# Another order of the first operations of a planned attention and MoE kernel, with 48 casts, copies and squares moved between ACT and DVE

## The chip, the cores and the metric

The kernel runs on one core of a Trainium2 chip. A core has five engines that this text calls PE (matrix multiplication), DVE (vector), ACT (scalar), POOL and SP. Each runs its own list of instructions strictly in the order in which the program gives them, and waits where an instruction needs a result that another engine or a transfer has not delivered. SP only issues transfers between HBM and on-chip memory. The metric is the time of one execution on the device in microseconds, as a median of several runs.

## The reference, cut to what matters

A linear attention with random features, and behind it a gated product with weights `w_a`, `w_b` and `w_out`:

```python
batch, n_heads, seq, head_dim, n_features = 8, 8, 576, 64, 128
n_tokens, d_model, d_ff = 4608, 512, 1536

def phi(x):
    proj = np.einsum('bhsd,md->bhsm', x, omega)
    sq = np.sum(x * x, axis=-1, keepdims=True) / 2.0
    h = proj - sq
    h = h - np.max(h, axis=-1, keepdims=True)
    return np.exp(h) / np.sqrt(m)
q_p, k_p = phi(q * scale), phi(k * scale)
kv = np.einsum('bhsm,bhsd->bhmd', k_p, v)
z = np.sum(k_p, axis=2)
num = np.einsum('bhsm,bhmd->bhsd', q_p, kv)
den = np.einsum('bhsm,bhm->bhs', q_p, z)[..., None] + 1e-06
x = num / den                      # then 4608 tokens x 512
out = ((x @ w_a) * (x @ w_b)) @ w_out
```

The weights come as 64-bit numbers, everything else as 32-bit.

## The kernel before

**Units.** The attention is cut into 32 units, one per batch and pair of heads; names end in the batch and the pair, so that `sm_0_1` belongs to batch 0, pair 1. A unit loads `X` (features in rows) and `natk`, `natq` (tokens in rows). `square_sums` (L557) squares a `nat` tile in place on ACT (L560) and sums it on DVE (L562). In the first pair of heads the squares come from `X` itself (L611) and PE sums them (L616). PE projects with `om` into `ppk` and `ppq` (L574), DVE takes maxima (L627) and forms the biases `sm` (L634, L635), and ACT computes the exponentials `hk` and `hq` (L640).

**The first four units** go through `tok_tail` (L964): PE transposes `hq` into `pq` (L957), a copy brings that to `qT`, PE forms `pkv` (L980) and `pn` (L994), DVE divides (L999 to L1006) into `x32t` and `tails`, PE transposes `x32t` into `px` (L1013), and `split` (L519) makes two halves of the result: `x` high, a cast (`copier`, L392), and `x` low, the subtraction of that cast (`subber`, L404). Each matrix product of the MoE is three PE products of such halves. Later units get their denominators through POOL and a small trip through HBM (`z_sums`, L792), and their transposition through another (`turn`, L881).

**Weights.** `convert` (L436) turns each 64-bit piece `raw` into 32-bit high and low halves: two ACT steps (L446, L448), one DVE step (L450), a cast that may be done by ACT (L396) or DVE (L398), and a subtraction on DVE (L404). There are 36 pieces, 24 of `wa` and `wb` and 12 of `wo`. The `raw` tiles share their memory with tiles that are used later or earlier, so a load has to wait until the last reader of the former tile is done.

**MoE.** The first two batches go through `moe_block` (L1232): for each of 12 steps, PE computes `pa` and `pb` (L1250, four groups of three products each over `x_0` to `x_3`), ACT copies `pa` to `a`, DVE multiplies (L1258) and splits the product into `ghl` high and low, and PE adds four groups of output products `o` (L1060). Batches from the third on use sums of weights and activations with seven products in place of eight (L1343, L1353).

**The order.** Nothing is written in the order in which it runs. The functions describe operations to a `Graph` (L60), each with a cost per engine that may do it, a due number and the tiles it reads and writes. `plan` (L313) runs a list scheduling of all engines and of the transfers, gives each operation one engine and each tile one place in memory, and returns the operations sorted by their planned start. The kernel then issues them in that sequence, so that each engine's list and SP's are cut out of one row of 5637 operations. What an instruction must wait for is worked out from the tiles when it is issued.

Of the kernel before, what the change touches and what calls it, by code (L numbers as in the profile page):

```python
# [352 lines left out]
def tile_attention_moe(ctx: ExitStack, tc: tile.TileContext, kqt, kqtt, kqn, kqnt, vx, omst, idn, wab, wout, out):  # L356
    nc = tc.nc
# [106 lines left out]
    for n, (kind, i, w) in enumerate(units):  # L464
        pr = 4000 + n * 4000 / len(units)
# [91 lines left out]
    def square_sums(src, sq, n, nm, pr, b, alloc_sq):  # L557

        for nat, o, part in src:
            g.op({"ACT": act(n * D)}, lambda e, nat=nat: nc.scalar.activation(nat.ap[:], nat.ap[:], AF.Square, scale=SQ),  # L560
                 r=[(nat, None)], w=[(nat, None)], prio=pr, margin=0 if b < 2 else CFG["LOAD"])
            g.op({"DVE": dve(n * D)}, lambda e, nat=nat, o=o: nc.vector.tensor_reduce(o(), nat.ap[:], axis=X, op=ALU.add),  # L562
                 r=[(nat, None)], w=[(sq, part)], alloc=[sq] if part in (0, None) else [], prio=pr)
# [529 lines left out]
    class Out7:  # L1093
# [26 lines left out]
        def product(self, key, A, W, prio, end, part=None):  # L1120

            n = self.n[key] = self.n.get(key, -1) + 1
            free = key in (1, 0)
            pb = spare[key] if free else self.acc[key]
            begin, stop = (key == 1 or n == 0), (key == 1 or end)

            def go(e):
                for t in range(2) if part is None else (part,):
                    for j, (ai, wi) in enumerate(((0, 0), (0, 1), (1, 0))):
                        nc.tensor.matmul(pb.ap[:, t], A[0](ai)[:, t * P:(t + 1) * P], W[0](wi), start=begin and t == j == 0, stop=stop and t == 1 and j == 2)  # L1130
            g.op({"PE": mm(6 if part is None else 3, HM)}, go, r=[*A[1], *W[1]], w=[(pb, 0), (pb, 1)] if part is None else [(pb, part)],
                 alloc=[pb] if n == 0 and not free else [], prio=prio)
            return pb
# [324 lines left out]
    for b in range(B + 1):  # L1458
# [3 lines left out]
        else:  # L1462
            if b == B:

                for hp in range(NHP):
# [3 lines left out]
                         prio=-20, nbytes=P * SM * 4)  # L1469
# [6 lines left out]

    order = g.plan()
    with tc.manual_schedule():  # L1480
        for o in order:
            for b in o.alloc:
# [70 lines left out]
```

## Time and profile before

| what | value |
|---|---|
| median of 3 runs | 1042.24 µs (1042.18 to 1042.42) |
| the profiled execution's own time | 1041.62 µs |
| its span from first to last instruction | 1039.8 µs |
| mean granted TensorE clock | 0.998 |
| POOL busy | 114.0 µs (11%) |
| transfers | 314.44 MB, 302 GB/s on average |
| largest share of the chain that ended last | PE, 79% |
| next in that chain | DVE 8%, ACT 1% |

The share of busy time says how much of the span an engine had an instruction running. PE's ends are modelled, so that a busy PE isn't PE at its peak. Idle time in a row stands in front of the instruction that ended it, with the engine or transfer that had been waited for.

### The profile page before, as it was taken

The page shows a single profiled execution, that of the slowest core. Times are in us where ns is not written, and L with a number is a line of the kernel's source. Part 1 is how long each engine was busy: PE and PEld are TensorE (multiplying, and loading weights), DVE is VectorE, ACT ScalarE, POOL GpSimd, SP SyncE. Part 2 cuts the span into 40 slices and gives each one's busy share as a digit, 9 for nine tenths or more (in the row PEclk, how much of TensorE's full clock was granted, in tenths as well). Part 3 has the DMA queues.
Part 4 walks back from the last instruction along what each step waited for, and adds up shares of the span by engine and source line. Part 5 has one row for each costly group of instructions (what it writes and reads, how often), then busy time and mean ns, then how long its engine had stood idle before and what let it go on. Part 6 is the DMA issues. An engine that isn't in the chain of part 4 may idle for free.

```text
span 1039.8 us, 26266 instructions
## 1 busy us (share of the span) xinstructions
PE 1024.4 (99%) x9902; PEld 897.0 (86%) x9902; DVE 887.3 (85%) x2212; ACT 598.4 (58%) x1656; POOL 114.0 (11%) x181
## 2 busy tenths in 40 slices
PE   9899999999999999999999999999999999999998
PEld 7677777777788888988888888888899899999998
DVE  6999999899999888878887978888876579998766
ACT  8997798677665665566565656665454123332211
POOL 0032211120111111111101111111110000000000
PEclk9999999999999999999999999999999999999999
DMA  9877879989899998999989988989888888899981
GB/s 352 308 281 239 285 242 307 304 331 317 298 349 363 307 317 294 315 330 313 306 275 351 310 300 296 339 303 309 272 288 268 268 320 313 318 344 341 371 303 47
DMA packets 123665, 314.44 MB, mean 302 GB/s; under 512 B 17681, under 2 KB 40977, under 8 KB 123537
## 3 DMA queue, kind: packets, MB, share of 16 engines
q1 hardware_dynamic: 122656, 312.10, 86.5%
q8 instruction: 78, 1.28, 0.5%
q10 hardware_dynamic: 880, 0.66, 0.2%
q14 instruction: 51, 0.41, 0.1%
HBM read 255.52 MB, written 57.18 MB: 301 GB/s over the span
## 4 chain that ended last, share of the span: by engine, by line
PE 79%; DVE 8%; ACT 1%; issue 1%; DVEq 0%; ACTq 0%
PE p L1343 39%; PE o L1060 19%; PE o_P L1130 5%; PE pa L1250 3%; PE pb L1250 3%; PE pkv L849 3%; PE pm L917 2%; PE ppk L594 1%; PE p L594 1%; DVE sm L627 1%; DVE c L1353 1%; PE p L1130 1%; DVE zero L868 1%; PE ppk L574 1%; PE ppke L574 1%
## 5 line engine op out<-in xcount | busy, mean ns | idle before, releaser
L1353 DVE TENSOR_TENSOR c<-p,c 128x512 f32<-128x512 f32 (+1 forms) x336 | 207.7, 618 | 67.9 <-PE p L1343 59.4
L1060 PE MATMUL o<-wo,ghl 128*128 128x512 f32 x1008 | 258.5, 397 | 0.4 <-DVE ghl L404 0.3
L1060 PEld LDWEIGHTS o<-wo,ghl 128*128 128x128 f32 x1008 | 181.0, 188 | 39.9 <-issue 4.7
L1343 PE MATMUL p<-Sa,t 128*128 128x256 f32 x1008 | 132.6, 281 | 0.0
L1343 PEld LDWEIGHTS p<-Sa,t 128*128 128x128 f32 x1008 | 124.6, 188 | 0.4 <-issue 0.2
L802 POOL TENSOR_TENSOR z<-hk 128x256 f32<-128x256 f32 x56 | 44.5, 795 | 607.7 <-ACT hk L640 431.3
L396 ACT CAST ghl<-c 128x512 fp32r<-128x512 f32 (+1 forms) x75 | 42.5, 579 | 100.5 <-DVE c L1403 80.9
L878 ACT ACTIVATE hq<-hq,dn 128x128 f32<-128x128 f32 x224 | 71.1, 392 | 29.1 <-DVE dn L874 28.9
L868 DVE CUSTOM_DVE_ANT_0 zero<-hq,zb 128x128 bf16<-128x128 f32 x224 | 79.5, 355 | 4.9
L1250 PE MATMUL pa<-x,wa 128*128 128x512 f32 x288 | 75.9, 406 | 3.6 <-ACT wa L396 2.0
L1343 PE MATMUL p<-Sb,bq 128*128 128x256 f32 x504 | 74.1, 283 | 0.0
L1343 PE MATMUL p<-x,t 128*128 128x256 f32 x504 | 74.0, 282 | 0.0
L1250 PE MATMUL pb<-x,wb 128*128 128x512 f32 x288 | 73.3, 398 | 0.4 <-DVE a L1258 0.4
L1343 PE MATMUL p<-Sb,t 128*128 128x256 f32 x504 | 73.5, 282 | 0.0
L396 ACT COPY c<-p 128x256 f32<-128x256 f32 x84 | 31.3, 372 | 73.0 <-PE p L1343 62.3
L1343 PEld LDWEIGHTS p<-x,wa 128*128 128x128 f32 x504 | 64.9, 188 | 7.2 <-DVE c L1353 3.7
L1343 PE MATMUL p<-x,wa 128*128 128x256 f32 x504 | 68.2, 283 | 2.0 <-DVE c L1353 1.0
L1250 PEld LDWEIGHTS pa<-x,wa 128*128 128x128 f32 x288 | 53.6, 191 | 19.0 <-ACT a L396 2.2
L640 ACT ACTIVATE hq<-hq,sm 128x128 f32<-128x128 f32 x192 | 65.4, 392 | 7.4 <-DVE sm L635 6.0
L1343 PEld LDWEIGHTS p<-x,wb 128*128 128x128 f32 x504 | 64.6, 188 | 3.8 <-DVE c L1353 0.6
L1343 PE MATMUL p<-x,wb 128*128 128x256 f32 x504 | 67.7, 282 | 0.1
L1343 PEld LDWEIGHTS p<-x,t 128*128 128x128 f32 x504 | 65.8, 189 | 1.6 <-DVE c L1353 0.4
(209 smaller groups left out, 2019.6 us busy)
## 6 DMA issues: line engine op xcount, KB each, us to landing
t<-td SPq DMA_DIRECT2D x168, 512.0 KB
wo<-wod SPq DMA_DIRECT2D x96, 512.0 KB
bq<-bd SPq DMA_DIRECT2D x84, 256.0 KB
qdr<-qd SPq DMA_DIRECT2D x112, 160.0 KB
hq<-qdr SPq DMA_DIRECT2D x28, 640.0 KB
X<-in_kqt_dram SPq DMA_DIRECT2D x30, 512.0 KB
raw<-in_wab_dram SPq DMA_DIRECT2D x24, 512.0 KB
td<-ts SPq DMA_DIRECT2D x24, 512.0 KB
```

The costliest lines, as they stand in the source:

```text
L396: nc.scalar.copy(o(), i())
L574: nc.tensor.matmul(pps[w].ap[half, c * M:c * M + M], x()[rows, c * P + D * t:c * P + D * t + D], om.ap[rows], start=True, stop=True)
L640: g.op({"ACT": 392}, lambda e, c=c, w=w, to=to, at=at: nc.scalar.activation(to.ap[:, at + c], src[w](c), AF.Exp, scale=SC, bias=sm.ap[:, 2 ...
L802: g.op({"POOL": pool2(n)}, lambda e: nc.gpsimd.tensor_tensor(o(), a(), c(), op=ALU.add), r=r, w=w, alloc=list(al), prio=pri, deps=zload[-1 ...
L849: nc.tensor.matmul(pkv.ap[D * j + d:D * j + d + Q, 0:M], vb.ap[:, vc, d:d + Q], c(), start=(n == 0), stop=(n == 4))
L868: g.op({"DVE": 413}, lambda e, c=c, j=j, rr=rr, qc=qc: nc.vector.tensor_tensor_reduce(out=junk.ap[rr], in0=qc(), in1=zb.ap[rr, j], scale=1 ...
L878: g.op({"ACT": 392}, lambda e, c=c, src=src: nc.scalar.activation(hq.ap[:, c], src(), AF.Copy, scale=dn.ap[:, c:c + 1]), r=[sd, (dn, None) ...
L1060: nc.tensor.matmul(po.ap[:], ghl.ap[:, gi, t * P:(t + 1) * P], wo.ap[:, wi], start=(n == 0 and i == 0), stop=(n == NF - 1 and i == 2))
L1130: nc.tensor.matmul(pb.ap[:, t], A[0](ai)[:, t * P:(t + 1) * P], W[0](wi), start=begin and t == j == 0, stop=stop and t == 1 and j == 2)
L1250: nc.tensor.matmul(pb.ap[:], wt.ap[:, wi, c], xs[c].at(xi), start=(c == 0 and i == 0), stop=(c == NC4 - 1 and i == 2))
L1343: nc.tensor.matmul(pb.ap[:, half], wcol(wi, c), xc(xi, c), start=n == 0, stop=n == 5)
L1353: g.op({"DVE": dve(n)}, lambda e: nc.vector.tensor_tensor(c4.ap[:, o], pb.ap[:, half], y(), op=ALU.add), r=[*((pb, k) for k in range(half. ...
```

## The change

Two tables of numbers and a function are added, and the sequence that the planner returns goes through that function. `OTHER` names places in the planner's sequence and an engine for each: 26 operations go from ACT to DVE, and 22 from DVE to ACT. They are the casts of weights (`convert`), the copies of `qT`, casts of `ghl`, copies of finished outputs, and the two squares of L611. `AFTER` has 1411 pairs; a pair (i, j) puts the operation at place i of the planner's sequence right behind the one at place j. Operations that aren't named keep their sequence. The highest place named is 2115, and the last 3311 of the 5637 operations stand where they stood. Places in memory are those the planner gave.

`square_sums` also gets a variant for POOL, which runs only where an operation has POOL as its engine. `OTHER` names DVE and ACT alone, so it runs nowhere. Line numbers grow by 25 to 30: L627 of before is L657 now, L562 is L590, L404 is L429, L398 is L423, L450 is L475, L611 is L641 (642 on DVE), L1250 is L1280 and L1060 is L1090.

```diff
+OTHER = ((27,"DVE"),(37,"DVE"),(99,"DVE"),(100,"DVE"),(131,"ACT"),(136,"DVE"),(169,"DVE"),
...
+AFTER = ((6,8),(5,9),(16,5),(15,20),(14,15),(13,24),(18,13),(37,40),(48,42),(57,45),(61,57),
...
+def arranged(order):
+
+    for i, e in OTHER:
+        order[i].eng = {e: 0}
+    moved = {i for i, _ in AFTER}
+    follow = {}
+    for i, j in AFTER:
+        follow[j] = i
+    got = []
+
+    def put(i):
+        while i is not None:
+            got.append(i)
+            i = follow.pop(i, None)
+    put(follow.pop(-1, None))
+    for i in range(len(order)):
+        if i not in moved:
+            put(i)
+    return [order[i] for i in got]
...
-            g.op({"ACT": act(n * D)}, lambda e, nat=nat: nc.scalar.activation(nat.ap[:], nat.ap[:], AF.Square, scale=SQ),
-                 r=[(nat, None)], w=[(nat, None)], prio=pr, margin=0 if b < 2 else CFG["LOAD"])
-            g.op({"DVE": dve(n * D)}, lambda e, nat=nat, o=o: nc.vector.tensor_reduce(o(), nat.ap[:], axis=X, op=ALU.add),
+            s = g.op({"ACT": act(n * D)}, lambda e, nat=nat: nc.scalar.activation(nat.ap[:], nat.ap[:], AF.Square, scale=SQ) if e == "ACT" else
+                     nc.gpsimd.tensor_tensor(nat.ap[:], nat.ap[:], nat.ap[:], op=ALU.mult),
...
-    order = g.plan()
+    order = arranged(g.plan())
```

DVE's list near its start, where unit 1 ends and unit 2 begins, before (`sm_1` and `sm_2` are the biases of pairs 1 and 2, `rd_00` the first division):

```order
L627 TENSOR_REDUCE sm_1_307<-ppk_14_335 128x4
L627 TENSOR_REDUCE sm_1_307<-ppq_14_336 128x4
L634 SCALAR_TENSOR_TENSOR sm_1_307<-sm_1_307,sq_1_324 128x2x4
L627 TENSOR_REDUCE sm_1_307<-ppq_10_304 128x4
L627 TENSOR_REDUCE sm_2_416<-ppk_20_412 128x4
L627 TENSOR_REDUCE sm_2_416<-ppq_20_413 128x4
L999 TENSOR_SCALAR rd_00_437<-pn_00_436 128x5
```

The same place of DVE's list now:

```order
L657 TENSOR_REDUCE sm_1_281<-ppq_14_324 128x4
L657 TENSOR_REDUCE sm_1_281<-ppk_14_323 128x4
L423 COPY qT_0_273<-pq_01_390 128x384
L590 TENSOR_REDUCE sq_2_401<-natk_2_153 128x8
L423 COPY qT_0_273<-pq_02_396 128x384
L657 TENSOR_REDUCE sm_2_412<-ppk_20_408 128x4
L657 TENSOR_REDUCE sm_2_412<-ppq_20_409 128x4
L1029 TENSOR_SCALAR rd_00_430<-pn_00_429 128x5
```

Ahead of the first maximum of unit 2 there now stand two copies of `qT` that ACT did before, and a sum of squares that stood further back.

PE's list in the first MoE batch, around the fifth step (`pa_4`, `pb_4`), before; `o_0` to `o_3` are the four outputs, and the number behind `ghl` is the step it comes from:

```order
L1060 MATMUL o_0_1098<-wo_1154,ghl_2_1315 128x512 x3
L1060 MATMUL o_1_1106<-wo_1154,ghl_2_1315 128x512 x3
L1060 MATMUL o_2_1118<-wo_1154,ghl_2_1315 128x512 x3
L1060 MATMUL o_3_1159<-wo_1154,ghl_2_1315 128x512 x3
L1250 MATMUL pa_4_1467<-x_0_530,wa_1255 128x512 x3
L1250 MATMUL pa_4_1467<-x_1_713,wa_1255 128x512 x3
L1250 MATMUL pa_4_1467<-x_2_829,wa_1255 128x512 x3
L1250 MATMUL pa_4_1467<-x_3_935,wa_1255 128x512 x3
L1250 MATMUL pb_4_1499<-x_0_530,wb_1345 128x512 x3
```

The same place now:

```order
L1280 MATMUL pb_4_1469<-x_1_732,wb_1334 128x512 x3
L1280 MATMUL pa_4_1399<-x_2_833,wa_1331 128x512 x3
L1090 MATMUL o_3_1087<-wo_1313,ghl_3_1441 128x512 x3
L1280 MATMUL pb_4_1469<-x_2_833,wb_1334 128x512 x3
L1090 MATMUL o_1_1251<-wo_1225,ghl_2_1316 128x512 x3
L1280 MATMUL pa_4_1399<-x_3_929,wa_1331 128x512 x3
L1090 MATMUL o_0_1095<-wo_1313,ghl_3_1441 128x512 x3
L1280 MATMUL pb_4_1469<-x_3_929,wb_1334 128x512 x3
```

Output groups of two steps stand singly between the groups of `pa` and `pb`, which alternate; some outputs of step 3 stand ahead of the end of step 4's first products, and before they stood behind all of them.

SP's list around the load of the fifteenth weight piece, before (`raw_972`) and now (`raw_1123`):

```order
L407 DMA raw_972<-in_wout_dram 128x512
L407 DMA xtd<-xts_571 128x4x64
L407 DMA X_1_978<-in_kqt_dram 128x1024
L407 DMA natq_1_984<-in_kqn_dram 128x512
L407 DMA raw_996<-in_wab_dram 128x512
```

```order
L432 DMA raw_1073<-in_wout_dram 128x512
L432 DMA raw_1121<-in_wab_dram 128x512
L432 DMA raw_1123<-in_wout_dram 128x512
L432 DMA X_1_1125<-in_kqt_dram 128x1024
L432 DMA zdr_87<-zx_0_1188 8x32
L432 DMA zb_0_1214<-zdr_87 128x256
```

`X_1_978` of before is `X_1_1125` now. The load `raw_1121` (the twentieth piece) now stands ahead of both; before it stood 15 rows behind the fifteenth.

More of the change, by code (lines that the diff above doesn't have):

```diff
@@ L42 @@
 CFG = dict(PORT=0.5, EDF=("DVE", "ACT", "POOL"), STEP=15000, LOOK=60000, NOISE=(200, 600), CHOSEN=((858009,0,387055,152612,0,0,0,715321,0,0,680034,0,0,0,0,780129,689749,0,892332,0,0,84647,0,0,0,0,0,0,0,0,0,0,0,0,0,0,0,0,0,0,0,0,0,0,0,0,0,0,0,0,0,0,0,0,0,0,0,0,0,0,0,0,0,0,0,0,0,0,0,0),), ZS=800, ZB=(300, 1600, 3600), ZD=(300, 1600, 3100), HQ=(1100, 2600, 3600), BACK2=(300, 1100, 2600), TW=(), XL=["v0", "v1", "Xt0", "ht2", "hq0"], OWR=["raw0", "raw1"], ONE=((7, 1),), SAFE=500, OWN=16, OWNU=(), HOLD=1000, TG=1, G4=4, WAIT=150, RAW=600, FAST=(0, 1, 2, 3), JOIN0=False, WARM=8, HROOM=["w0", "u1", "w1", "u2", "w2", "u3"], H=3, TURN=(7,), BACK=1500, AT=2, GATES=(-4, -1, 2, 5), SQPE=4, MARGIN=1200, LOAD=1100, SUMS=1000, NATS=(1, 2, 3), CONV=(28000, 2600))
+OTHER = ((27,"DVE"),(37,"DVE"),(99,"DVE"),(100,"DVE"),(131,"ACT"),(136,"DVE"),(169,"DVE"),(219,"DVE"),(224,"ACT"),(242,"DVE"),(259,"ACT"),(269,"DVE"),(270,"ACT"),(284,"DVE"),(352,"ACT"),(354,"ACT"),(355,"DVE"),(402,"DVE"),(447,"ACT"),(449,"ACT"),(475,"ACT"),(494,"ACT"),(560,"ACT"),(562,"ACT"),(674,"ACT"),(683,"DVE"),(707,"ACT"),(708,"ACT"),(736,"ACT"),(801,"DVE"),(813,"DVE"),(973,"ACT"),(976,"DVE"),(1006,"DVE"),(1070,"ACT"),(1081,"DVE"),(1142,"DVE"),(1218,"DVE"),(1331,"DVE"),(1403,"ACT"),(1498,"ACT"),(1709,"DVE"),(1848,"ACT"),(1862,"DVE"),(1866,"DVE"),(1939,"DVE"),(1950,"ACT"),(2049,"DVE"),)
@@ L559, in square_sums, with total @@
         for nat, o, part in src:
-            g.op({"ACT": act(n * D)}, lambda e, nat=nat: nc.scalar.activation(nat.ap[:], nat.ap[:], AF.Square, scale=SQ),
-                 r=[(nat, None)], w=[(nat, None)], prio=pr, margin=0 if b < 2 else CFG["LOAD"])
-            g.op({"DVE": dve(n * D)}, lambda e, nat=nat, o=o: nc.vector.tensor_reduce(o(), nat.ap[:], axis=X, op=ALU.add),
-                 r=[(nat, None)], w=[(sq, part)], alloc=[sq] if part in (0, None) else [], prio=pr)
+            s = g.op({"ACT": act(n * D)}, lambda e, nat=nat: nc.scalar.activation(nat.ap[:], nat.ap[:], AF.Square, scale=SQ) if e == "ACT" else
+                     nc.gpsimd.tensor_tensor(nat.ap[:], nat.ap[:], nat.ap[:], op=ALU.mult),
+                     r=[(nat, None)], w=[(nat, None)], prio=pr, margin=0 if b < 2 else CFG["LOAD"])
+            def total(e, nat=nat, o=o, s=s):
+                nc.vector.tensor_reduce(o(), nat.ap[:], axis=X, op=ALU.add)
+                if "POOL" in s.eng:
+                    nc.gpsimd.tensor_scalar(o(), o(), SQ2, 0.0, op0=ALU.mult, op1=ALU.add)
+            g.op({"DVE": dve(n * D)}, total, r=[(nat, None)], w=[(sq, part)], alloc=[sq] if part in (0, None) else [], prio=pr)
     def four(nm, b, pri, x, xdep, dst, c0, sm, sq, al, deps, mg, more):
```

1 line of the change is left out of this document (added).

## The prediction

> **What bounds the kernel now.** I read the totals first and then the table of windows, since the change ends near 450 µs and an average over the whole span says little about that stretch. A window's columns are the stretch, its length, the busy time and instruction count of PE, PEld (weight loads), DVE, ACT and POOL, the granted clock, the DMA share and GB/s.
>
> ```profile
> PE 1024.4 (99%) x9902; PEld 897.0 (86%) x9902; DVE 887.3 (85%) x2212; ACT 598.4 (58%) x1656; POOL 114.0 (11%) x181
> ...
> 0.00:25.00 25.00, 22.96 (x441) 17.79 (x445) 17.18 (x44) 20.71 (x65) 1.19 (x11) 1.00 0.93 351
> 25.00:50.00 25.00, 21.19 (x319) 16.81 (x311) 23.05 (x59) 24.19 (x63) 0.40 (x2) 0.93 0.83 308
> 50.00:75.00 25.00, 24.31 (x220) 18.80 (x220) 24.79 (x51) 24.51 (x63) 6.06 (x8) 1.00 0.87 305
> 75.00:100.00 25.00, 24.64 (x194) 19.01 (x193) 24.77 (x76) 20.01 (x54) 8.13 (x10) 1.00 0.66 209
> 100.00:125.00 25.00, 24.64 (x239) 18.38 (x242) 24.77 (x58) 18.80 (x52) 5.54 (x6) 1.00 0.83 289
> 125.00:450.00 325.00, 322.84 (x3037) 267.38 (x3025) 293.58 (x781) 223.77 (x623) 47.54 (x72) 1.00 0.91 313
> 450.00:1040.00 590.00, 583.82 (x5488) 538.80 (x5476) 479.14 (x1148) 266.40 (x742) 45.09 (x72) 1.00 0.86 298
> ```
>
> PE is idle for 2.04 + 3.81 = 5.85 µs up to 50, for 0.69 + 0.36 + 0.36 = 1.41 from 50 to 125, and for 2.16 from 125 to 450, 9.4 in all. The change takes no work off PE, so the order can win only idle time and time at a low clock. The low clock of 0.93 sits in one place:
>
> ```profile
> 36.00:38.00 2.00, 1.18 (x32) 0.94 (x32) 1.66 (x3) 2.00 (x7) 0.20 (x1) 1.00 0.96 381
> 38.00:40.00 2.00, 0.51 (x18) 0.37 (x14) 1.83 (x3) 2.00 (x6) 0.00 (x0) 1.00 0.67 254
> 40.00:42.00 2.00, 1.49 (x4) 0.97 (x5) 2.00 (x6) 2.00 (x5) 0.00 (x0) 0.85 0.05 20
> 42.00:44.00 2.00, 2.00 (x6) 1.51 (x6) 1.93 (x6) 2.00 (x5) 0.00 (x0) 0.50 0.87 295
> 44.00:46.00 2.00, 2.00 (x9) 1.59 (x8) 1.92 (x5) 2.00 (x5) 0.00 (x0) 0.80 0.57 229
> ```
>
> Two poorly filled windows (1.18 and 0.51 of 2 µs) are followed by 2 × (0.15 + 0.50 + 0.20) = 1.7 µs of lost clock. With the 9.4 that makes **11.1 µs, the ceiling** of what the order can bring, unless PE's matmuls also stand closer than their modelled ends show. In these windows DVE and ACT are full, and DVE stays full (24.8 of 25) to 125. So up to about 125 µs I take the time from DVE's list: PE waits for what DVE and ACT hand over.
>
> **The change part by part.** *DVE's first work.* The timeline gives start, duration, instruction, and the idle time before it with what ended it.
>
> ```profile
> 3.97 0.63 ACT L611 ACTIVATE x<-X 128x512 f32<-128x512 f32 x1 [1.00 <-DMA X<-in_kqt_dram]
> 6.26 0.63 ACT L611 ACTIVATE x<-X 128x512 f32<-128x512 f32 x1 [0.84 <-DMA X<-in_kqt_dram]
> 5.38 0.69 DVE L627 TENSOR_REDUCE sm<-ppk 128x4 f32<-128x512 f32 x1 [4.44 <-PE ppq L574]
> 17.17 0.69 DVE L627 TENSOR_REDUCE sm<-ppk 128x4 f32<-128x512 f32 x1 [1.51 <-PE ppq L574]
> 20.39 0.55 DVE L398 COPY qT<-pq 128x384 f32<-128x384 f32 x1
> 20.85 0.67 DVE L562 TENSOR_REDUCE sq<-natk 128x8 f32<-128x512 f32 x1
> 21.44 0.68 DVE L562 TENSOR_REDUCE sq<-natq 128x8 f32<-128x512 f32 x1
> ```
>
> DVE idles until 5.38. Now its first row is a square that ACT did at 3.97, as soon as X had landed; DVE so has work from 3.97, which wins 5.38 − 3.97 = 1.4. Against it stands SP's new order, with one more load of 128x512 (0.26 MB) ahead of the second half of X. At the 351 GB/s of the first window that is 0.75 µs. The half landed by 6.26, and DVE wants it for its second square after one square, two maxima and two small steps, near 3.97 + 1.8 + 0.4 = 6.2. So it costs between 0 (if that load lands beside others) and 0.75; I take 0.4, the middle, since neither row is nearer. *First work: +1.0.*
>
> *The hole at 17.17.* DVE waits 1.51 for PE there. Its new list has two copies of `qT` and a sum of squares in front of this reduction. From start to start a copy takes 20.85 − 20.39 = 0.46 and a sum 21.44 − 20.85 = 0.59, together 1.51. Useful work fills the hole: *+1.5*, between 0 (if `pq` isn't there yet) and 1.51; I take the upper end because PE's `pq` product stands ahead in its list.
>
> *Waits for ACT's casts.*
>
> ```profile
> 31.93 0.69 DVE L404 TENSOR_TENSOR x<-px,x 128x512 fp32r<-128x512 f32 x1 [0.26 <-ACT x L396]
> 38.16 0.69 DVE L404 TENSOR_TENSOR x<-px,x 128x512 fp32r<-128x512 f32 x1 [0.48 <-ACT x L396]
> 40.02 0.42 DVE L398 CAST wb<-raw 128x512 fp32r<-128x512 f32 x1
> 40.36 0.16 DVE L999 TENSOR_SCALAR rd<-pn 128x5 f32<-128x5 f32 x1
> 47.86 0.69 DVE L404 TENSOR_TENSOR x<-px,x 128x512 fp32r<-128x512 f32 x1 [0.37 <-ACT x L396]
> 50.54 0.68 DVE L404 TENSOR_TENSOR wa<-raw,wa 128x512 fp32r<-128x512 f32 x1
> ```
>
> They are 0.26 + 0.48 + 0.37 = 1.1 µs. ACT's list ahead of the last of these casts is 15 rows shorter and 5 longer, so ACT comes earlier, but DVE comes earlier too. Between 0 and 1.1 I take half, *+0.6*.
>
> *Length of DVE's list.* Counted in the two lists with 0.59 for a sum, maximum, square or subtraction, 0.46 for a copy and 40.36 − 40.02 = 0.34 for a cast: ahead of the subtraction at 50.54 stand 4.7 µs of work that were not there and 5.0 fewer, *+0.3*. If reading `pq` and `raw` on DVE beside busy ACT costs more than these rows, it is between −1 (a fifth on 4.7) and +0.3; I keep +0.3.
>
> At 50 µs that makes 1.0 + 1.5 + 0.6 + 0.3 = **3.4**, of PE's 5.85 idle and 1.7 of clock, so there is room for it.
>
> The clock alone can spoil this. By the rows above, windows with PE a quarter to a half busy were enough, and PE was never idle for more than 2.0 µs in a row, as its waits show:
>
> ```profile
> 37.12 1.39 PE L994 MATMUL pn<-kvz,qT 128*64 128x66 f32 x40 [0.82 <-ACT kvz L396]
> 40.51 3.95 PE L1250 MATMUL pa<-x,wa 128*128 128x512 f32 x9 [2.00 <-ACT wa L396]
> ```
>
> If the gap at 40.51 shrinks with the earlier hand-over, the dip goes too and PE can follow DVE's full gain. The Trainium skill ("TensorE: Matmul & The Clock Gate", Part 1, "What's actually happening") puts the half clock behind an idle window of about 3.4 µs that runs freely. By that rule the dip would not hang on this 2.00 µs gap and could come back at another place; the trace here speaks for the row, with a dip behind a shorter gap, and the sum by the rule would be 1.7 lower.
>
> *From 50 to 125.* Ahead of the first low half of `ghl` in the fourth step DVE's list has 12 rows more (5.3 µs) and 20 fewer (9.2), 3.9 shorter; in the seventh step it is 2.7 shorter (6.0 against 8.7). DVE being full there, PE could be handed its data that much earlier, but PE has only 1.41 of idle left: *+1.4*, from 0 (PE is bound by itself) to 1.4. I take the upper end as DVE's surplus is over twice as large.
>
> *From 125 to 450.* PE's idle 2.16 in many small waits; its operations are moved up to 354 µs, by at most 16 places. Between −2.2 (as much new idle as there was) and +2.2; half, *+1.0*, since the moves put single output groups between waiting products. Behind that nothing is moved.
>
> *Sum:* 3.4 + 1.4 + 1.0 = 5.8. The profiled execution took 1041.62 (span 1039.8 and 1.8 around it), so 1035.8; the median of the runs stands 0.62 higher: **1036.4**.
>
> **The rivals.** *ACT takes over as the bound.* ACT has 24.51 of 25 busy from 50 to 75, and between 51 and 100 its list grows by 6 rows net.
>
> ```profile
> 62.15 0.65 ACT L396 CAST wa<-raw 128x512 fp32r<-128x512 f32 x1
> 62.70 0.71 ACT L448 ACTIVATE raw<-raw 128x512 int32<-128x512 uint32 x1
> 63.30 1.24 ACT L446 ACTIVATE raw<-raw 128x512 f32<-128x512 f32 x2
> 83.02 0.66 ACT L446 ACTIVATE raw<-raw 128x512 f32<-128x512 f32 x1 [1.26 <-DMA raw<-in_wab_dram]
> ```
>
> At 62.70 − 62.15 = 0.55 each, that is 3.3: of the 3.4 nothing much is left, and with the late 1.0 the median is 1042.24 − 1.1 = 1041.1. Against it: from 0 to 51 ACT's list is 2.8 shorter, and from 75 on ACT has 5 of 25 free.
>
> *The slower one: SP's list stops behind one load.* SP issues in order. The load of the twentieth piece waits for the last reader of the memory that it reuses, the low half of the fourth `wa` piece, which is the last of these four:
>
> ```profile
> L404 DVE TENSOR_TENSOR wa<-raw,wa x4: 676/688/692, 40.5 to 62.8; 128x512 fp32r<-128x512 f32 x4
> ...
> 47.30 0.42 SPq L407 DMA_DIRECT2D raw<-in_wout_dram  x1
> 63.55 0.36 SPq L407 DMA_DIRECT2D raw<-in_wab_dram  x1
> 78.27 0.33 SPq L407 DMA_DIRECT2D raw<-in_wab_dram  x1
> ```
>
> It was issued at 63.55, right after that subtraction ended (62.8 + 0.7). Now the fifteenth piece, issued at 47.30 before and read by ACT at 63.30, stands behind it, and so do X of the next batch and the transfers of `z`. The load issued at 78.27 kept ACT waiting until 83.02, so one lands about 4.7 µs after its issue. If the subtraction still ends at 63.5, the fifteenth piece is there at 63.5 + 0.4 + 4.7 = 68.6, 5.3 after ACT wanted it; ACT stands still, and with it every `ghl` behind it. DVE would have gained nothing by then; less the late 1.0 that is +4.3, a median of 1046.5. It begins to cost when the subtraction ends after 63.30 − 4.7 − 0.4 = 58.2. I expect 63.5 − 3.4 (gained at 50) − 2.5 (DVE's list ahead of it is shorter by that) = 57.6, close to the edge, but ACT's reader also stands 9 rows further back in ACT's list, about 9 × 0.55 = 5 µs of cover.
>
> *A smaller gain:* the hole at 17 and the first work only move the wait to ACT or to X; then 0.6 + 0.3 + 1.4 + 1.0 = 3.3, and 1038.9. *A larger gain:* the dip goes and the small waits too, up to the ceiling of 11.1: 1031.1. That the change does nothing can be excluded: 1411 of 5637 places differ in the lists.
>
> **How the numbers follow.** About 0.2% (2.1 µs) is what a measurement of this kernel can tell from no change. Forecast, a gain of 4 to 9 µs: 0.50. Larger gain, above 9: 0.11. Smaller, 2.1 to 4: 0.15. ACT as the bound, within 0.2%: 0.13. SP's stop, slower by more than 0.2%: 0.11. Faster so has 0.50 + 0.11 + 0.15 = 0.76. The range has to leave out no more than 2 in 10: from the ceiling, 1031.0, to 1043.0, which takes in the smaller gain and ACT's case, and leaves out most of the slower case and of what might lie beyond the ceiling.
>
> **What would show it.** DVE's first row after the memset starts near 4.0; no wait above 0.3 µs is left near 17; the first `pa` product of the MoE starts before 38.5, and the window 42 to 44 shows clock 1.00; PE's idle from 25 to 50 falls from 3.81 to under 2; from 450 on PE's busy and idle time stay as they were, only earlier. The slower rival would show as SP waiting before the load of the twentieth piece and ACT waiting for `raw` near 60 µs; ACT's case as DVE and PE waiting for ACT's `ghl` or `wa` casts from 50 to 75. The prediction is wrong if PE's time is lost between matmuls that stand close already, so that the idle that goes comes back as longer spacing, or if DVE's copies and casts take longer beside ACT than in the rows used.

## The result, and the profile after

The changed kernel takes 1054.17 µs (median of 4 runs, 1052.92 to 1054.74) against 1042.26 before, a ratio of 1.0112 with a 95% interval of 1.0095 to 1.0130. It is 11.9 µs slower, and the prediction had said 5.8 µs faster. The profiled execution took 1052.92 µs (span 1051.1), the shortest of the four.

The windows of the changed kernel, with the columns of before:

```profile
0.00:25.00 25.00, 22.93 (x414) 17.40 (x418) 19.34 (x50) 19.96 (x64) 1.13 (x10) 1.00 0.93 345
25.00:50.00 25.00, 23.94 (x373) 19.49 (x368) 24.63 (x65) 25.00 (x69) 0.95 (x3) 1.00 0.84 312
50.00:75.00 25.00, 24.75 (x257) 19.28 (x253) 23.85 (x55) 23.57 (x58) 8.93 (x13) 1.00 0.63 218
75.00:100.00 25.00, 23.84 (x154) 17.09 (x156) 23.40 (x63) 23.08 (x58) 4.46 (x7) 1.00 0.80 270
100.00:125.00 25.00, 24.35 (x249) 18.29 (x250) 24.26 (x66) 19.54 (x55) 4.59 (x7) 1.00 0.86 292
125.00:450.00 325.00, 314.94 (x2891) 257.99 (x2890) 287.82 (x756) 215.62 (x599) 46.19 (x72) 0.99 0.88 304
450.00:1040.00 590.00, 588.97 (x5539) 543.52 (x5539) 481.94 (x1160) 269.93 (x754) 45.60 (x72) 1.00 0.88 303
```

From 25 to 50 PE idles 1.06 µs where it idled 3.81, and the clock is full. From 75 on it goes the other way: 1.81 idle from 75 to 125 (0.72 before), and 10.06 from 125 to 450 (2.16 before). DVE, which had 24.8 of 25 from 50 to 125, has 23.4 to 24.3 now. The engines are *less* busy and the work takes longer, so waits have been added.

**Position at equal PE work.** To see where, I matched the two traces operation by operation (both hold the same 1320 groups on PE), gave each kind of group the start-to-start time that its fastest tenth has in the kernel before, and summed these up along each kernel's own list. The table says how much later (+) or earlier (−) each kernel begins the same amount of PE work than the kernel before, with the first projection of each trace put at the same time; up to 0.9 µs of the first column is a start that differs from one execution to the next (e2, e6 and e16 begin with the old lists). Each row is one execution; e15's was 1.3 µs longer than the median of its runs, the change's 1.3 shorter. Kernels of the experiments are in it too.

| before is at | 25 | 55 | 80 | 125 | 200 | 250 | 450 | 1030 |
|---|---|---|---|---|---|---|---|---|
| the change | 0.8 | −5.8 | −5.7 | −3.1 | 0.1 | 7.0 | 9.7 | 11.2 |
| e1: new order for 400 operations | 1.0 | −5.5 | −1.2 | −1.1 | −0.4 | −0.4 | −0.1 | 1.6 |
| e2: new order behind 400 | 0.9 | 0.4 | 0.4 | 2.1 | 5.3 | 13.3 | 16.1 | 15.8 |
| e3: swaps alone | 0.1 | 0.4 | 2.3 | 2.3 | 3.9 | 5.7 | 7.3 | 7.1 |
| e4: order alone | 6.9 | 2.0 | 5.8 | 11.5 | 19.2 | 24.5 | 28.1 | 29.8 |
| e5: SP's list by readiness | 1.7 | −4.6 | −4.5 | −1.8 | 6.4 | 12.1 | 23.3 | 25.4 |
| e6: new order behind 1000 | 0.9 | 0.4 | 0.4 | 0.4 | 2.6 | 5.9 | 8.3 | 8.0 |
| e7: new order for 1000 | 1.8 | −4.7 | −4.7 | −2.2 | 6.0 | 6.0 | 6.8 | 8.3 |
| e8: new order for 300 | 1.3 | −2.2 | −2.1 | −3.2 | −3.1 | −3.2 | −2.8 | −1.4 |
| e13: eleven rows ahead | 1.2 | −5.3 | −5.2 | −2.8 | 2.8 | 7.8 | 12.3 | 13.7 |
| e14: 116 rows ahead | 1.4 | −5.1 | −3.1 | 3.1 | 9.6 | 16.4 | 24.6 | 26.0 |
| e15: the change, DVE light | 1.0 | −5.5 | −5.2 | −4.0 | −2.2 | 2.1 | 1.8 | 3.1 |
| e16: the old order, DVE light | 0.9 | 0.0 | 0.0 | −1.6 | −1.9 | −2.4 | −2.6 | −3.1 |

The change is 5.8 µs ahead at 55, holds that to 80, and then loses 15.4 until 450, and another 1.5 slowly behind it, where nothing was moved.

**What the loss looks like.** All waits of PE from 125 to 450 (engine, line and tile waited for, µs in total, times, longest), before:

```profile
PE p L1343 <- ACT hk L396: 0.8, 1, 0.8
PE pa L1250 <- ACT a L396: 0.7, 1, 0.7
PE o L1060 <- DVE ghl L404: 0.3, 1, 0.3
PE ppq L594 <- ACT k L396: 0.2, 1, 0.2
```

and now:

```profile
PE pb L1280 <- DVE a L1288: 2.5, 3, 1.9
PE ppk L624 <- DVE x L429: 1.7, 2, 1.0
PE ppk L604 <- DVE x L429: 1.4, 1, 1.4
PE ppq L604 <- DVE x L429: 1.4, 2, 0.9
PE p L1373 <- ACT hk L421: 0.7, 1, 0.7
PE ppq L624 <- ACT k L421: 0.7, 1, 0.7
PE p L1373 <- DVE Sa L429: 0.5, 1, 0.5
PE pa L1280 <- ACT a L421: 0.4, 1, 0.4
PE o L1090 <- DVE ghl L429: 0.4, 1, 0.4
```

That is 2.0 µs in 4 waits against 9.7 in 13, and no single one carries it. PE's idle time grows by 7.9 in this stretch and a half-clock stretch near 250 takes 1.7, together 9.6 of the 12.8 µs that the table has from 125 to 450. The other 3.2 stand in neither: the same groups of products take longer from start to start. PE's ends are modelled, and where those 3.2 lie wasn't looked into. The largest wait, 1.94 at 248.90, shows the manner. The product `a` of DVE releases the bank that the next `pb` writes to. The timelines of DVE and PE in the changed kernel:

```profile
240.62 0.29 DVE L898 CUSTOM_DVE_ANT_0 zero<-hq,zb 128x128 bf16<-128x128 f32 x1 [2.31 <-ACT hq L670]
...
247.82 0.29 DVE L898 CUSTOM_DVE_ANT_0 zero<-htq,zb 64x128 bf16<-64x128 f32 x1
248.04 0.08 DVE L898 DVE_READ_ACCUMULATOR2_ANT dn<- 64x1 f32 x1
248.15 0.69 DVE L1288 TENSOR_TENSOR a<-pb,a 128x512 f32<-128x512 f32 x1
...
246.46 0.49 PE L1090 MATMUL o<-wo,ghl 128*128 128x512 f32 x1 [0.38 <-DVE ghl L429]
248.90 0.97 PE L1280 MATMUL pb<-x,wb 128*128 128x512 f32 x3 [1.94 <-DVE a L1288]
```

DVE first stands 2.31 for `hq` and `zb` (put down to ACT, whose first `hq` of this unit was done at 236.4; the load of `zb`, issued at 233.2, is the likelier releaser, as its semaphore rose at 240.48), then works through rows of the denominators, and comes to the product 4 µs after its inputs are there. PE then loses the 1.94 and a half-clock stretch behind it. On the chain of waits that ended last, the pieces of transfers sum to 50 µs from 60 to 350 (17 to 130, 9 to 200, 24 to 350). Before there is none, as far as that chain goes back, to 104. By line, for the window 200 to 350, before and now:

```profile
by line: PE p L1343 19.0%; PE o L1060 16.0%; PE pa L1250 8.8%; PE pb L1250 7.4%; PE pkv L849 4.1%; issue 3.9%; DVE zero L868 3.2%; DVE wr L1281 2.9%; PE pm L917 2.9%; DVE ts L404 2.9%; DVE sm L627 2.8%; ACT hq L640 2.4%; ACT hq L878 1.8%; D
```

```profile
by line: PE p L1373 7.4%; DVE zero L898 7.0%; DMA td<-ts 6.0%; issue 5.7%; DMA qdr<-qd 5.6%; PE o L1090 5.6%; DMA zb<-zdr 4.5%; DMA X<-in_kqt_dram 3.6%; ACT hq L908 3.5%; DVE ts L429 3.3%; PE pb L1280 3.2%; PE pa L1280 3.0%; DVE sq L590 2.7
```

Before, the chain runs mostly through PE. Now it hops between DVE, PE, transfers and ACT, and none of these works through.

### The profile page after: what moved, and what is told of

The parts are those of the page before. It is cut to its first block, busy times and chain, and to the rows that moved or that the text cites. A ratio compares the mean times of both kernels' runs of the same rounds, so it can differ in the third digit from the quotient of the medians.

```text
span 1051.1 us, 26233 instructions
## 1 busy us (share of the span) xinstructions
PE 1030.2 (98%) x9902; PEld 899.3 (86%) x9902; DVE 891.2 (85%) x2216; ACT 597.1 (57%) x1652; POOL 111.8 (11%) x181
## 4 chain that ended last, share of the span: by engine, by line
PE 70%; DVE 15%; DMA 8%; ACT 4%; issue 2%; SPq 1%; DVEq 0%; ACTq 0%
PE p L1373 37%; PE o L1090 17%; PE o_P L1160 4%; PE pkv L879 2%; DMA raw<-in_wab_dram 2%; DVE zero L898 2%; PE pm L947 2%; PE ppk L624 1%; PE p L624 1%; PE pb L1280 1%; DMA zb<-zdr 1%; DVE raw L475 1%; DVE c L1383 1%; DMA qdr<-qd 1%; PE pa L1280 1%
## 5 line engine op out<-in xcount | busy, mean ns | idle before, releaser
L1090 PE MATMUL o<-wo,ghl 128*128 128x512 f32 x1008 | 265.2, 397 | 0.4 <-DVE ghl L429 0.4
L1090 PEld LDWEIGHTS o<-wo,ghl 128*128 128x128 f32 x1008 | 180.9, 188 | 39.5 <-issue 4.3
L1373 PE MATMUL p<-Sa,t 128*128 128x256 f32 x1008 | 135.0, 282 | 0.5 <-DVE Sa L429 0.5
L1373 PEld LDWEIGHTS p<-Sa,t 128*128 128x128 f32 x1008 | 127.0, 189 | 1.5 <-DVE Sa L429 0.7
L1280 PE MATMUL pa<-x,wa 128*128 128x512 f32 x288 | 81.6, 405 | 1.0 <-ACT a L421 1.0
L1280 PE MATMUL pb<-x,wb 128*128 128x512 f32 x288 | 79.3, 399 | 3.2 <-DVE a L1288 2.5
L1373 PE MATMUL p<-Sb,t 128*128 128x256 f32 x504 | 74.1, 283 | 0.0
L1373 PE MATMUL p<-x,t 128*128 128x256 f32 x504 | 73.8, 282 | 0.0
L1373 PE MATMUL p<-Sb,bq 128*128 128x256 f32 x504 | 73.7, 282 | 0.0
L1373 PEld LDWEIGHTS p<-x,wa 128*128 128x128 f32 x504 | 65.0, 189 | 7.3 <-DVE c L1383 4.0
L1373 PE MATMUL p<-x,wa 128*128 128x256 f32 x504 | 68.6, 283 | 1.9 <-DVE c L1383 1.0
L670 ACT ACTIVATE hk<-hk,sm 128x128 f32<-128x128 f32 x184 | 63.2, 392 | 10.7 <-DVE sm L665 6.9
L1280 PEld LDWEIGHTS pb<-x,wb 128*128 128x128 f32 x288 | 52.8, 188 | 18.6 <-DVE a L1288 4.6
L1373 PEld LDWEIGHTS p<-x,wb 128*128 128x128 f32 x504 | 64.8, 188 | 3.8 <-DVE c L1383 0.7
L1373 PE MATMUL p<-x,wb 128*128 128x256 f32 x504 | 67.7, 282 | 0.1
```

The lines of the kernel that those rows point to most:

```text
L670: g.op({"ACT": 392}, lambda e, c=c, w=w, to=to, at=at: nc.scalar.activation(to.ap[:, at + c], src[w](c), AF.Exp, scale=SC, bias=sm.ap[:, 2 ...
L1090: nc.tensor.matmul(po.ap[:], ghl.ap[:, gi, t * P:(t + 1) * P], wo.ap[:, wi], start=(n == 0 and i == 0), stop=(n == NF - 1 and i == 2))
L1280: nc.tensor.matmul(pb.ap[:], wt.ap[:, wi, c], xs[c].at(xi), start=(c == 0 and i == 0), stop=(c == NC4 - 1 and i == 2))
L1373: nc.tensor.matmul(pb.ap[:, half], wcol(wi, c), xc(xi, c), start=n == 0, stop=n == 5)
```

## The experiments

### Early or late part, swaps or order

Kernel e1 takes the new order for its first 400 operations only, e2 for all the others:

```diff
+    was = {i: order[i].eng for i, _ in OTHER}
     for i, e in OTHER:
         order[i].eng = {e: 0}
...
+    head = set(got[:400])
+    for i in was: order[i].eng = order[i].eng if i in head else was[i]
-    return [order[i] for i in got]
+    return [order[i] for i in got[:400] + sorted(set(got) - head)]
```

> The new order (with the engines that it gives) for its first 400 operations, which end near 57 us; behind them all operations in the old order with their old engines. Compared at equal PE work, the change was 5.7 us ahead of before at 55 us and 9.7 us behind at 450. Theory A (the loss sits in the new lists from 60 us on, above all in SP's, where loads now stand behind waiting transfers): the 5.7 stays, 1036 to 1038. Theory B (whatever is won early is given back, since weights and loads don't come earlier and DVE is full to 125 us): 1041 to 1043. Theory C (the early order leaves something behind that costs later): 1046 or more.

```diff
+    head = set(range(400))
+    for i in was: order[i].eng = was[i] if i in head else order[i].eng
-    return [order[i] for i in got]
+    return [order[i] for i in sorted(head) + [i for i in got if i not in head]]
```

> The first 400 operations in the old order with their old engines, the rest as the change has it. Theory A: the loss of 5.7 + 9.7 = 15.4 us between 55 and 450 is there without the early gain, near 1057. Theory B: the loss was the gain given back plus some, 1046 to 1052. Theory C: near 1042, since what harms is left out.

e1 took 1043.09 (ratio 1.0012, interval 1.0002 to 1.0022), e2 1056.50 (1.0137, 1.0122 to 1.0153). e1 lies at the upper edge of theory B's range, e2 at theory A's figure. The table says more than the times. e2 starts with the old lists, has no early gain, and loses 15.7 from 55 to 450, as much as the change. **So the loss belongs to the new lists behind the 400th operation, with or without the early gain**; that settles theory C against the early part. In e1 the gain of 5.5 is there until 65 µs and 4.3 of it goes in one place, at the seam, where DVE, ACT and PE stand together (PE 2.60 for `a`, and a half-clock stretch). So theory A's 1037 doesn't come, and what takes the gain is the seam, not the weights and loads of theory B.

The two halves of the change alone: e3 has `return order` in place of the last line, e4 an empty loop over `OTHER`.

```diff
-    for i, e in OTHER:
+    for i, e in ():
```

> The 48 changes of engine alone, all lists in the old sequence. Theory A: the swaps matter little beside SP's list, 1040 to 1046. If the engine swaps make the loss (theory D: work on ACT or DVE where it is waited for), 1050 or more.

> The new sequence alone, each operation on its old engine. Theory A: most of the loss stays, 1050 to 1058. Theory D (the swaps make the loss): 1036 to 1044.

e3 took 1048.68 (1.0063, 1.0048 to 1.0078) and e4 1072.18 (1.0290, 1.0265 to 1.0315). Both miss: e3 lies between the two theories, e4 far above both, and theory D falls with it. Swaps alone cost 6.4 µs, the order alone 30, and together 11.9. The two prices don't add up, so neither half has a price of its own. A likely reason, argued and not shown, is that the order is written for these swaps, and without them the engines meet rows whose work stands on another engine.

### Is it SP's list?

> The lists of PE, DVE, ACT and POOL as the change has them, row for row. Only SP's list differs: a transfer is put where its memory and its data were ready in the trace of the change, but not before the time at which it was issued in the kernel before; 394 operations move in the sequence, and X of unit 2 of the third batch, issued at 195.1 us after 37 us behind waiting transfers, comes ahead near 160. Theory A (SP's list makes the loss): at least half of the 15.4 us come back, 1047 or less. Theory E (the loss is in the lists of DVE, ACT and PE, and transfers only show it): 1051 to 1056.

The edit is another table `AFTER`, with which the lists of the four engines stay as they are:

```diff
-AFTER = ((6,8),(5,9),(16,5),(15,20),(14,15),(13,24),(18,13),(37,40),(48,42),(57,45),(61,57),
...
+AFTER = ((3,0),(2,3),(8,2),(7,1),(16,9),(5,10),(19,13),(20,14),(27,15),(26,17),(24,26),
...
```

e5 took 1069.16 (1.0265, 1.0248 to 1.0282): 15 µs *slower* than the change, against both theories. The likely reason is that transfers that were ready came out ahead of those that were needed. The chain from 120 to 140 µs of e5 has this piece (start, length, what):

```profile
122.00 8.68 DMA raw<-in_wab_dram
```

A weight piece was issued at 122.00 and landed 8.68 µs later (the 4.7 of the prediction was another `raw` load of the same size, of before). Theory A falls in the form in which it was put: letting SP issue what is ready doesn't bring the loss back, it adds to it. That a load lands late because of what was issued just ahead of it would fit, but no run here takes that apart.

### Where along the way?

e6 and e7 are e2 and e1 with 1000 in place of 400, e8 is e1 with 300.

> The first 1000 operations in the old order with their old engines (to about 157 us), the rest as the change has it. At equal PE work the change went from 1.8 us ahead at 160 to 9.7 behind at 450. If that part loses by itself: 1042.2 + 11.5 = 1054. If it loses only because the part ahead of it left the engines in another state: 1046 or less.

> The new order for its first 1000 operations, to about 158 us, the old one behind it. The change stood 1.8 us ahead there: near 1040.4 if that is kept, 1043 to 1046 if the seam costs as much as the 4.3 us that the seam at 400 operations cost.

> The new order for its first 300 operations, to about 42 us, the old one behind it. There the change stood 2.4 to 4.4 us ahead, and the half-clock stretch at 41 to 45 us was gone. Kept: 1038 to 1040. Given back, as theory B has it (weights and loads don't come earlier): 1041.5 to 1043.

e6 took 1051.03 (2 runs), e7 1048.43 (2 runs), e8 1041.18 (10 runs; 0.9992, 0.9983 to 1.0002). The rows behind 1000 operations (157 µs) lose 7.9 by themselves, between the two forecasts; e7 lies above both forecasts and loses 5.2 on the way from 55 to 160 µs, and 5.5 at its seam. In the trace of e8 PE is 2.1 µs ahead at 60 and 3.2 at 250, with the old lists from 42 µs on. **So the early gain is real, and part of it can be kept by the old order**, which theory B had excluded. In time that doesn't show: 1041.18 lies between the two forecasts and isn't told from before, as e8 gives back 1.4 µs between 450 and 1030 in a part that has the old lists (see the last section).

e11, e12, e17 and e18 put the seam at 340, 460, 260 and 320.

> The new order for its first 340 operations, to about 48 us, the old one behind it. At 300 operations 2.1 to 3.1 us were kept up to 450 us; the change stands 5 us ahead at 50. If the seam is clean: 1038 to 1039.5. If it costs what it cost at 400 operations (4.3 us): 1042 to 1043.

> The new order for its first 460 operations, to about 67 us, the old one behind it; the change stands 5.6 us ahead there. Clean seam: 1038. A seam as at 400 operations: 1042 to 1043.

> The new order for its first 260 operations, to about 36 us, the old one behind it. The hole at 17 us and the early start are in, and the gain that PE shows only from 36 us on has to come out of DVE's lead of 3 us there. If DVE's lead is what counts: 2 to 4 us faster, 1038 to 1040. If the rows between 36 and 42 us are needed for it: 1042 or more.

> The new order for its first 320 operations, to about 45 us, the old one behind it. The seam at 300 kept 3.1 us, that at 340 none. Something between, 1039 to 1042, if the cost of a seam grows with how far the new lists have put work off; 1042 to 1044 if it costs as much as at 340.

They took 1043.56, 1044.70, 1043.14 and 1043.28; at 450 µs they stand 0.2 and 1.2 behind, and 0.1 and 1.3 ahead. None beats e8, and none is faster than before; e17 and e18 lie in the slower of their two forecasts, e11 and e12 above both. Of seven seams only e8's kept more than 1.3 µs up to 450, so its place is in part luck. What a seam costs doesn't grow evenly with its place.

### Are the trips through DRAM too short?

DVE's wait for `zb` suggested that the new lists leave the round trips of `z` and `hq` too little time. In e9 both are read back from the tile of the unit before:

```diff
-            lambda: zd.rearrange("c r -> (c r)").partition_broadcast(P))
+            lambda: (zdram[(u - 1) % 3] if u > 4 else zd).rearrange("c r -> (c r)").partition_broadcast(P))
...
-            lambda: qdr.rearrange("j r i n -> (j r) (i n)"))
+            lambda: (qdram[(u - 1) % 3] if u > 4 else qdr).rearrange("j r i n -> (j r) (i n)"))
```

> The change, but from the second unit of the second batch on, the sums zb and the turned hq are read back from the DRAM tile that the unit before it wrote, so that neither read waits for its own unit's write to land (output differs from the reference: wrong denominators and queries from there on). Theory G (the new lists from 80 us on leave the two trips through DRAM 8 to 9 us where the old left 10 to 14, so that DVE and ACT, and SP's whole list, stand in wait for their landings): about 30 of the 55 us that DMA has on the chain of waits from 60 to 350 us belong to these trips, and 4 to 9 us of the 12 come back, 1045 to 1050. Theory E (the loss is in the order of DVE, ACT and PE among themselves): less than 2 us, 1052 or more.

> The same cut of the two trips in the kernel before (old order, old engines; output differs in the same way). In its trace DVE's first read of zb never waits and DMA is not on the chain of waits from 60 to 350 us. Theory G: within 1 us of before, 1041.2 to 1043. If the trips cost the old order as much as the new one: 1036 to 1039.

e9 took 1052.72 (1.0106, 1.0091 to 1.0121), 1.4 less than the change and within its spread; e10 took 1041.82, as before. By the forecast that speaks for theory E and against theory G. But the edit did less than meant, and the same row shows it:

```profile
241.08 0.53 DVE L898 CUSTOM_DVE_ANT_0 zero<-hq,zb 128x128 bf16<-128x128 f32 x1 [1.96 <-DMA zb<-zdr]
```

DVE still waits 1.96 for `zb` here: what is long is the load itself, not the wait for the unit's own write. So this says only that the writes' landing isn't the cause. The loads' share stays open.

### Single late rows?

For each wait of PE I looked up how early its inputs were there before, and now. Eleven of them had 0.3 to 9 µs to spare and have almost none. e13 puts these eleven rows 1 to 11 places ahead in DVE's and ACT's lists, e14 does it for 116; both by another table `AFTER`, in which SP's, POOL's and PE's lists stay as they are.

> The change with eleven operations put ahead in their own engine's list, 1 to 11 rows each, to where their inputs are ready in the trace of the change: on DVE the low halves of two weight pieces, three products of pb and a, two x low halves; on ACT three copies of pa and one cast of x. In the kernel before PE found each of them done 0.3 to 9 us early, in the change 0.05 to 1.3 us early, and the lost PE time in front of their readers sums to about 10 us, with the half-clock stretch at 250 us near 12. Theory H (the 15 us are lost where single results that PE needs stand some rows too far back): 5 to 10 us come back, 1044 to 1049, and the half clock at 250 is gone. Theory E (DVE and ACT are short of time anyway, so that the rows that are passed come late in their place): less than 3 us, 1051 or more.

> The change with 116 operations of DVE and ACT between 58 and 360 us put ahead in their lists: all whose first PE reader came within 2 us and that had had a longer lead in the kernel before; each goes to where its inputs are ready, at most 4 us ahead of its reader. Theory H: as much as the eleven or more, 1041 to 1047. Theory E: less than 3 us or a loss, 1051 or more.

e13 took 1056.48 (1.0141, 1.0125 to 1.0157), e14 1068.15 (1.0252, 1.0234 to 1.0269): slower than the change by 2.3 and 14. Half of what e13 was to show did come: its clock is full at 250 µs, and of the eleven results only one (an `x` low half) is still late by the table of waits. Yet others are late in their place, the longest a wait of PE of 2.8 µs for a copy of ACT and one of 2.2 for an exponential. Theory H falls: to bring single late rows ahead doesn't remove the loss.

### Room on DVE

e15 takes DVE's maxima and sums of squares over a quarter of their columns from the second batch on, in the new order, and e16 does so in the old:

```diff
-                nc.vector.tensor_reduce(o(), nat.ap[:], axis=X, op=ALU.add)
+                nc.vector.tensor_reduce(o(), nat.ap[..., 0:D if b < 1 else 16], axis=X, op=ALU.add)
...
-                sm.ap[:, 0, w, sl], whole(), axis=X, op=ALU.max), r=held[w], w=[(sm, (c0, w))], prio=pri + w)
+                sm.ap[:, 0, w, sl], whole()[..., 0:M if b < 1 else 32], axis=X, op=ALU.max), r=held[w], w=[(sm, (c0, w))], prio=pri + w)
```

> The change, with DVE's maxima and sums of squares from the second batch on taken over a quarter of their columns (a quarter of the data; the output differs from the reference). Some 75 such rows of 0.6 us from start to start stand between 60 and 350 us; at about 0.2 each DVE gets some 30 us of room there. Theory E (the new lists lose because DVE is short of time and every row that is moved makes another late): with that room the 15 us mostly vanish, and this kernel is 6 us ahead to 3 us behind the same cut in the old order. Theory I (the waits come from the sequence itself, each engine standing at a row whose input comes late, whatever room DVE has): it stays 8 us or more behind.

> The same cut of DVE's maxima and sums in the kernel before (old order, old engines). PE is busy 98.9% from 60 to 350 us there, so that room on DVE can bring little: 1038 to 1042 in both theories.

e15 took 1043.86 (1.0014, 1.0002 to 1.0026) and e16 1038.59 (0.9968, 0.9957 to 0.9978), 5.3 µs apart where the full kernels are 11.9 apart. The windows 50 to 125 and 125 to 450 of e15:

```profile
50.00:125.00 75.00, 73.31 (x659) 55.67 (x658) 63.97 (x184) 67.89 (x175) 17.73 (x25) 1.00 0.78 266
125.00:450.00 325.00, 317.61 (x2944) 263.63 (x2943) 264.20 (x769) 216.89 (x608) 45.73 (x72) 1.00 0.90 312
```

DVE is busy 328.2 µs there and was 359.3 in the change (71.51 + 287.82), so it has 31 µs of room. With it the new order loses 7.0 from 80 to 450 instead of 15.4, and the old order gains 2.6, so that the two are 9.6 apart over this stretch. The 5.3 lie between the two forecasts. By the medians 6.6 of the 11.9 go, by the traces 5.8 of the 15.4: **about half of the loss, or somewhat less, answers to DVE's time, and the rest doesn't.** With 64.0 of 75 and 264.2 of 325 DVE is no longer full, and PE still idles 7.39 from 125 to 450. The shorter rows both leave DVE room and bring the maxima sooner to ACT; these two aren't told apart.

## Why the prediction was wrong

*DVE's first work (+1.0).* About right in size, by other parts:

```profile
4.38 0.69 DVE L642 TENSOR_TENSOR x<-X 128x512 f32<-128x512 f32 x1 [3.44 <-DMA X<-in_kqt_dram]
5.72 0.69 DVE L657 TENSOR_REDUCE sm<-ppk 128x4 f32<-128x512 f32 x1 [0.65 <-PE ppq L604]
```

DVE waits 3.44 and 0.65 here, and waited 4.44 and then 0.40 before, 0.75 more. The first row starts at 4.38, not 3.97, and behind it DVE waits for PE again, which the step left out. The later X need not come from the new list, which issues X first (at 0.74, and 0.75 before): PE's first projection started at 4.23 in the trace of before and at 4.40 to 4.75 in the five other kernels with the old start.

*The hole at 17 (+1.5).* Right, row by row:

```profile
15.79 0.55 DVE L423 COPY qT<-pq 128x384 f32<-128x384 f32 x1
16.25 0.67 DVE L590 TENSOR_REDUCE sq<-natk 128x8 f32<-128x512 f32 x1
16.84 0.55 DVE L423 COPY qT<-pq 128x384 f32<-128x384 f32 x1
17.60 0.69 DVE L657 TENSOR_REDUCE sm<-ppk 128x4 f32<-128x512 f32 x1 [0.20 <-PE ppq L604]
```

Of 1.51 a wait of 0.20 is left.

*The first 50 µs (3.4 in sum).* Measured 5.2, under-sized. DVE's part came: it was busy 43.97 of these 50 µs against 40.23, 3.7 more, and the step had counted 3.1 of waits. The first `pa` of the MoE starts at 38.07 (40.51 before), and the half clock at 41 to 45 is gone with the gap ahead of it:

```profile
38.00:40.00 2.00, 2.00 (x24) 1.39 (x23) 1.97 (x9) 2.00 (x5) 0.00 (x0) 1.00 0.59 176
40.00:42.00 2.00, 2.00 (x38) 1.69 (x29) 1.98 (x5) 2.00 (x6) 0.00 (x0) 1.00 0.98 371
42.00:44.00 2.00, 2.00 (x11) 1.64 (x10) 1.91 (x6) 2.00 (x5) 0.00 (x0) 1.00 0.99 346
```

I took 3.4 as what DVE gains and kept the 1.7 of the clock for the ceiling. Their sum, 5.1, is near what came, but in part by luck: in PE's own windows the idle time is 2.7 less and the clock gave 1.7, 4.4 in all, and whether the old start has that half clock differs between executions (last section).

*From 50 to 125 (+1.4).* Failed: from 5.2 ahead to 3.1 ahead, −2.1. The step reasoned that the shorter part of DVE's list ahead of `ghl` is a surplus. It was in part work put off: DVE's fourth low half of `ghl` starts at 80.73 (89.35 before), but its sixth low half of `wo` at 98.57 (91.14 before). That such rows are what PE then lost is argued, not shown; PE's idle time from 50 to 125 is only 0.65 above that of before.

*From 125 to 450 (+1.0, with −2.2 and +2.2 as its bounds).* This is the step that failed most: from 3.1 ahead to 9.7 behind, −12.8. The bounds were taken from PE's present idle time, and nothing but symmetry stood behind the lower one. In its place the runs show 7.9 µs of new idle time, 1.7 of half clock and 3.2 of longer spacing. The prediction had named the last as a sign of being wrong, and its sum has no term for any of the three. (The old 2.16 were not many small waits either: 2.0 of it are the four shown above.) PE's idle time bounds what a new order can win; **it doesn't bound what it can lose**, as there was none of the new waits in the old trace to read a price from. The same trace showed DVE at 293.6 of 325, PE at 322.8 and the transfers at 0.91 over that stretch: two engines and the transfers, all issued in order, all nearly full, and hardly a wait of PE. Every full kernel here that moves rows in it lost against before (e2, e4, e5, e6, e7, e9, e13, e14, and e3 with engines alone), by 6 to 30 µs. All are variants of one order; another one wasn't tried.

*The rivals.* The slower one priced 1046.5 by the load of the twentieth piece. It didn't happen: the timeline of SP has the two loads, the twentieth and the fifteenth piece, side by side,

```profile
55.33 0.33 SPq L432 DMA_DIRECT2D raw<-in_wab_dram  x1
55.71 0.43 SPq L432 DMA_DIRECT2D raw<-in_wout_dram  x1
```

3 µs ahead of 58.2, the point from which the rival would cost. ACT as the bound would have ended within 0.2%. The result lies beyond both, by no mechanism that the prediction had. That the change does nothing had been excluded with 1411 places that differ; 1411 is the number of operations moved, and 2280 places hold another operation.

*From 450 on, the same.* 1.5 µs were lost there as well, see the end.

**What stays open.** Shown is that the loss is made by the new lists behind some 400 operations, that issuing transfers as they are ready, reading past the write side of the two trips, or bringing late rows ahead doesn't bring it back, and that about half of it goes when DVE has room. What makes the rest stays open. Loads that land late may be part of it, but the chain of waits can't say: transfers have 67 µs of it from 60 to 350 in e15, more than the 50 in the change, which loses more. A kernel with lighter transfers wasn't tried, nor one with lighter work on ACT.

## What to carry to other kernels

Where several in-order queues are nearly full and nothing waits, the idle time in the trace is the ceiling for a gain, and says nothing on the loss: give the downside of a wholesale reorder a price of its own, from how many queues are full and how many rows move. Undo such a change by place (first part new, rest old, and the reverse) before asking which row is at fault: here it took two kernels to see that the first 55 µs won 5.5 and the rest lost 16. And work that is taken out of a full engine's list ahead of one reader isn't saved, it has to stand ahead of a later one.

## What the runs showed of the hardware

*A half clock behind a gap of 2 µs, or not.* In the changed kernel PE is idle for 0.38 and 1.94 µs near 247, and the clock falls behind it. In e8 PE is idle for 2.16 µs near 46, and the clock stays full. The clock records of the 20 traces tell the two apart. All 16 half-clock stretches between a kernel's start and its end last 3.41 µs or twice that, and within a trace they start whole multiples of 3.41 apart: in e5 at 180.34, 211.06 and 327.12, which is 9 and 43 of them. So a trace can be cut at these borders into windows of 3.41 µs. For the change:

```profile
246.91:250.32 3.41, 1.47 (x7) 1.20 (x7) 3.30 (x12) 1.12 (x4) 0.00 (x0) 1.00 0.70 258
250.32:253.73 3.41, 3.41 (x10) 2.62 (x9) 3.34 (x8) 3.35 (x13) 0.00 (x0) 0.50 0.74 197
```

For e8, whose gap lies in two windows:

```profile
43.52:46.93 3.41, 1.73 (x9) 1.04 (x7) 3.32 (x7) 3.41 (x9) 0.00 (x0) 1.00 0.71 217
46.93:50.34 3.41, 2.58 (x10) 1.82 (x11) 3.38 (x8) 3.41 (x11) 0.00 (x0) 1.00 0.92 343
```

PE is busy 43% of the window ahead of the half clock in the change, and 51% and 76% of the two in e8. Over all traces each half-clock stretch follows a window in which PE is busy 0 to 49%, and of the 6019 full-clock windows without one behind them five have less than half, 44 to 49%. So a gap of 2 µs brings the half clock or not by where it lies, and the border is near a half by PE's modelled ends. The half clock of before is such a case: e6 has the same lists and engines there and the same gap, 2.03 µs ahead of 41.75, but the gap is divided between two windows and the clock stays full (the lines show e6).

```profile
37.17:40.58 3.41, 1.71 (x43) 1.34 (x41) 2.89 (x5) 3.41 (x9) 0.20 (x1) 1.00 0.71 217
40.58:44.00 3.42, 2.25 (x9) 1.56 (x10) 3.40 (x8) 3.42 (x7) 0.00 (x0) 1.00 0.08 24
```

The Trainium skill ("TensorE: Matmul & The Clock Gate", Part 1, "What's actually happening") asks for an idle window of about 3.4 µs that runs freely. The 3.41 and the free running agree with the traces; that the window has to be idle doesn't, as PE was busy up to 49% of it. The prediction had set its row, a dip behind a gap of 2.00, against this rule; by these traces the gap counts only by its share of a window.

*A layout effect.* Between 450 and 1030 µs, where all lists are the same, the change loses 1.5 µs. The waits don't grow; each group of six products of L1373 takes 2 to 4 ns more. All 14 kernels whose first 260 operations or more stand in the new order lose 1.3 to 2.1 there against before, and the five that start with the old order lose nothing (−0.4 to 0.0), be their engines or tails new or not. The planner gives each tile a named place, but in the program a place gets its address where it is first used. So with the new start 852 or more of the 1794 on-chip tiles lie at other addresses, 1267 in the change, although the places are those of the planner; in the five it is 198 in e2 and none in the others. For the product of `Sa` and `t` from 450 to 1000 µs, before and in the change (busy µs, mean ns):

```profile
L1343 PE MATMUL p<-Sa,t 128*128 128x256 f32 x756 | 99.4, 280 | 0.0
```

```profile
L1373 PE MATMUL p<-Sa,t 128*128 128x256 f32 x756 | 100.8, 282 | 0.0
```

That the addresses are the reason is argued from this count, not shown: the new start with the old addresses wasn't run.
